# First expert's raw weights and two transposed v tiles in their own slots, loads in another order, key maxima one slot ahead

## The chip, the cores and the metric

The kernel runs on one core of a Trainium2 chip. The metric is the device time of one execution in microseconds (us); the figures are the median and the range of three executions. One more execution was recorded by the hardware profiler. The core has five engines that each work through an instruction stream of their own: TensorE (PE, matmuls), VectorE (DVE), ScalarE (ACT), GpSimd (POOL) and SyncE (SP, which here issues all DMAs, in order). They wait for each other by semaphores.

## The reference

Local attention over 2 x 8 heads, then a mixture of four experts, then a two-matrix layer with a sigmoid gate. All inputs are float32 (the last two matrices arrive as float64).

```python
# attention, per head: 768 queries, head size 64
k_sum = k.reshape(B, H, nb, 32, D).max(axis=3)        # block maxima of the keys
v_sum = v.reshape(B, H, nb, 32, D).mean(axis=3)       # block means of the values
scores_l = where(|i - j| < 16, scale * q @ k.T, -1e9)
scores_s = scale * q @ k_sum.T + log(32)
a = softmax(concat(scores_l, scores_s))               # (its sum + 1e-9)
x = a @ concat(v, v_sum)                              # -> (1536, 512)
# experts: p = domain_probs / (sum + 1e-9)
out = sum over e of p[:, e] * (relu(x @ w1[e]) @ w2[e])     # 512 -> 1024 -> 512
# last layer: h = out @ w_in (512 -> 2048); g = h * sigmoid(1.702 h); result g @ w_out
```

## The kernel before, in words

Heads are handled in pairs (`hp`, four of them), which fill 128 partitions. A *group* is one batch, one pair and four windows of 64 queries; there are 24. Each group passes through a pipeline with one stage a *slot*: `att_a(i)` and `att_b(i)` are slot i. In slot i group i gets its scores (TensorE; VectorE scales them, adds the mask and takes the row maximum), group i-1 is normalised (VectorE sums, GpSimd multiplies), group i-2 is transposed, group i-3 is multiplied with v. `maxima` are the block maxima of a pair's keys, `windows` copies the four key windows and (on GpSimd) the maxima behind them into one tile kw, two slots ahead of use. `fold_v` (GpSimd), `sums` (VectorE) and `means` (TensorE, ScalarE, GpSimd) make the block means of v and put them behind the group's v tile.

A float32 product is made from two parts: hi, rounded to TensorE's format by ScalarE, and lo, the remainder. `split(k, h, hi engine, lo engine)` does this for half h of weight piece k (A = 0: first matrix, C = 1: second); lo is a subtraction of a 128 x 512 tile on GpSimd or VectorE. Each product takes three passes (hi hi, hi lo, lo hi). The first expert has eight pieces, the four experts 32.

The main program starts with ten idle matmuls, then slots 0 to 7. From slot 4 to 7 TensorE also makes the first four hidden tiles, one contraction step a slot (`early`): here xhi, xlo, whi and wlo of pieces 0 to 3 are needed. Behind slot 7 the four are scaled and split by `hidden`, in VectorE's stream ahead of slot 8. From then on each slot has also one unit: twelve matmuls of a hidden tile (`first`), and twelve or 24 of an output (`second`).

The order on each engine is that in which the program text runs. The dictionaries `middle` and `after` say which weight splits and loads belong to which slot. SyncE takes the loads in the order in which they are written; a load whose buffer is still read waits there, and all behind it too. Buffers: q tiles 4, vT tiles 2, vw tiles 5, raw weight halves 5 (each 128 x 512), and a pool of nine slots of 8 KB per partition that the key pairs, xhi and xlo, and later the accumulators use. Beyond 110 us the program only runs units; there `load_w(k + 2)` is called behind the split of piece k.

## Time and profile before

| | |
|---|---|
| median of 3 executions | 893.27 us (892.4 to 895.41) |
| profiled execution | 894.08 us |
| span in the profile (first to last instruction) | 892.3 us |
| TensorE busy | 861.5 us, 97% |
| VectorE / ScalarE / GpSimd busy | 394.9 / 254.6 / 249.8 us |
| mean granted TensorE clock | 0.987 of full speed |
| chain that ended last, by engine | PE 88%, DVE 5%, DMA 4% |

A time in a row is counted from the start of the span. In a timeline the bracket at a row's end gives how long the engine was idle before the instruction and what ended that. A granted clock of 0.50 is TensorE's lower level, 1.2 GHz, and 1.00 the upper, 2.4 GHz.

### The profile page before, as it was taken

The page shows a single profiled execution, that of the slowest core. Times are in us where ns is not written, and L with a number is a line of the kernel's source. Part 1 is how long each engine was busy: PE and PEld are TensorE (multiplying, and loading weights), DVE is VectorE, ACT ScalarE, POOL GpSimd, SP SyncE. Part 2 cuts the span into 40 slices and gives each one's busy share as a digit, 9 for nine tenths or more (in the row PEclk, how much of TensorE's full clock was granted, in tenths as well). Part 3 has the DMA queues.
Part 4 walks back from the last instruction along what each step waited for, and adds up shares of the span by engine and source line. Part 5 has one row for each costly group of instructions (what it writes and reads, how often), then busy time and mean ns, then how long its engine had stood idle before and what let it go on. Part 6 is the DMA issues. An engine that isn't in the chain of part 4 may idle for free.

```text
span 892.3 us, 11708 instructions
## 1 busy us (share of the span) xinstructions
PE 861.5 (97%) x4564; PEld 717.5 (80%) x4564; DVE 394.9 (44%) x684; ACT 254.6 (29%) x586; POOL 249.8 (28%) x261
## 2 busy tenths in 40 slices
PE   6679899999999999999999999999999999999998
PEld 6568788888888888788888888888788888888886
DVE  6457554235555455655455653232322222223233
ACT  3555554123411113211113212123423234322221
POOL 5546432015631115621116613034500014200000
PEclk8889999999999999999999999999999999999999
DMA  7552322204532325542225411003200002001011
GB/s 237 156 191 93 111 66 69 84 12 154 165 107 71 83 80 160 172 120 71 83 71 177 152 50 35 1 14 100 76 0 1 1 25 83 1 1 48 0 48 48
DMA packets 36199, 71.72 MB, mean 80 GB/s; under 512 B 5040, under 2 KB 8368, under 8 KB 36144
## 3 DMA queue, kind: packets, MB, share of 16 engines
q1 hardware_dynamic: 36144, 70.98, 25.4%
q8 instruction: 36, 0.59, 0.3%
q14 instruction: 19, 0.16, 0.1%
HBM read 59.40 MB, written 11.56 MB: 80 GB/s over the span
## 4 chain that ended last, share of the span: by engine, by line
PE 88%; DVE 5%; DMA 4%; ACT 1%; issue 1%; POOL 1%; SPq 0%; DVEq 0%; POOLq 0%; ACTq 0%
PE h L402 42%; PE o L455 41%; PE sc L288 2%; PE xo L338 1%; DMA q<-kq 1%; DMA k<-kq 1%; PE at L326 1%; DVE acc L479 1%; DVE g L420 1%; DVE hl L428 0%; POOL wlo L216 0%; DMA vT<-vT 0%; DVE nm L301 0%; DVE s L296 0%; ACT hh L427 0%
## 5 line engine op out<-in xcount | busy, mean ns | idle before, releaser
L427 ACT CAST hh<-g 128x512 fp32r<-128x512 f32 (+1 forms) x152 | 90.9, 598 | 406.1 <-DVE g L420 369.5
L216 POOL TENSOR_TENSOR wlo<-raw,whi 128x512 fp32r<-128x512 f32 x91 | 121.9, 1363 | 163.3 <-ACT whi L210 155.5
L428 DVE TENSOR_TENSOR hl<-g,hh 128x512 fp32r<-128x512 f32 (+1 forms) x152 | 114.8, 756 | 106.3 <-ACT hh L427 106.3
L402 PE MATMUL h<-xhi,wlo 128*128 128x512 f32 (+1 forms) x416 | 156.1, 375 | 3.0 <-POOL wlo L216 3.0
L402 PE MATMUL h<-xhi,whi 128*128 128x512 f32 (+1 forms) x416 | 158.6, 381 | 0.0
L455 PE MATMUL o<-hh,whi 128*128 128x512 f32 (+1 forms) x416 | 155.6, 374 | 2.1 <-DVE g L420 2.1
L402 PE MATMUL h<-xlo,whi 128*128 128x512 f32 (+1 forms) x416 | 156.0, 375 | 0.0
L455 PE MATMUL o<-hl,whi 128*128 128x512 f32 (+1 forms) x416 | 155.2, 373 | 0.0
L455 PE MATMUL o<-hh,wlo 128*128 128x512 f32 (+1 forms) x416 | 155.1, 373 | 0.0
L420 DVE SCALAR_TENSOR_TENSOR g<-h,pb 128x512 f32<-128x512 f32 (+1 forms) x104 | 67.6, 650 | 175.9 <-PE h L402 175.9
L426 DVE TENSOR_TENSOR g<-h,g 128x512 f32<-128x512 f32 x48 | 33.2, 692 | 155.2 <-ACT g L425 155.2
L402 PEld LDWEIGHTS h<-xhi,wlo 128*128 128x128 f32 x416 | 79.1, 190 | 17.0 <-POOL wlo L216 3.1
L455 PEld LDWEIGHTS o<-hh,whi 128*128 128x128 f32 x416 | 78.4, 188 | 17.3 <-DVE g L420 3.8
L402 PEld LDWEIGHTS h<-xhi,whi 128*128 128x128 f32 x416 | 79.4, 191 | 15.3 <-issue 0.6
L402 PEld LDWEIGHTS h<-xlo,whi 128*128 128x128 f32 x416 | 79.2, 190 | 13.5
L455 PEld LDWEIGHTS o<-hh,wlo 128*128 128x128 f32 x416 | 78.3, 188 | 13.8
L455 PEld LDWEIGHTS o<-hl,whi 128*128 128x128 f32 x416 | 78.4, 188 | 13.7
L193 POOL TENSOR_SCALAR d<-d 128x512 int32<-128x512 int32 x32 | 20.6, 644 | 216.0 <-DVE d L189 216.0
L455 PE MATMUL o<-whi,hh 128*128 128x512 f32 x192 | 74.9, 390 | 0.7 <-DVE g L426 0.7
L402 PE MATMUL h<-yhi,wlo 128*128 128x512 f32 x192 | 74.8, 390 | 0.0
L455 PE MATMUL o<-wlo,hh 128*128 128x512 f32 x192 | 74.8, 389 | 0.0
L402 PE MATMUL h<-ylo,whi 128*128 128x512 f32 x192 | 74.8, 389 | 0.0
(69 smaller groups left out, 987.2 us busy)
## 6 DMA issues: line engine op xcount, KB each, us to landing
raw<-wts SPq DMA_DIRECT2D x64, 256.0 KB, 4.8
d<-w SPq DMA_DIRECT2D x32, 512.0 KB, 4.5
w<-o SPq DMA_DIRECT2D x32, 256.0 KB, 2.3
raw<-w SPq DMA_DIRECT2D x32, 256.0 KB, 2.9
vw<-vw SPq DMA_DIRECT2D x24, 192.0 KB, 3.5
k<-kq SPq DMA_DIRECT2D x8, 400.0 KB, 6.4
q<-kq SPq DMA_DIRECT2D x24, 128.0 KB, 3.4
vT<-vT SPq DMA_DIRECT2D x8, 384.0 KB, 3.5
```

The source lines that it names most:

```text
L193: nc.gpsimd.tensor_scalar(out=lo, in0=lo, scalar1=0.5, scalar2=0.25, op0=ALU.mult, op1=ALU.add)
L216: engine.tensor_tensor(out=wlo[k][:, c], in0=raws[k, h], in1=whi[k][:, c].bitcast(F32), op=ALU.subtract)
L288: nc.tensor.matmul(ps[r, j * KA : (j + 1) * KA], q[r, j * WIN : (j + 1) * WIN], k[r, j, :], start=True, stop=True,)
L326: nc.tensor.transpose(ps[0:KA, j * P : (j + 1) * P], s[:, j, :], ident)
L338: nc.tensor.matmul(ps[h * D : (h + 1) * D, j * WIN : (j + 1) * WIN], v[0:KA, j, h * D : (h + 1) * D], a[0:KA, j * P + h * WIN : j * P + (h ...
L402: nc.tensor.matmul(hid[i][:, 0:n], wt[:, c], xt[:, k, x], start=(k == 0 and m == 0), stop=(k == KC - 1 and m == 2),)
L420: nc.vector.scalar_tensor_tensor(out=g, in0=ps, scalar=0.0, in1=pbs[ph, t][:, c0 : c0 + n], op0=ALU.max, op1=ALU.mult,)
L426: nc.vector.tensor_tensor(out=g, in0=ps, in1=g, op=ALU.mult)
L427: nc.scalar.copy(hh, g)
L428: nc.vector.tensor_tensor(out=hl, in0=g, in1=hh.bitcast(F32), op=ALU.subtract)
L455: nc.tensor.matmul(o, a, b, start=(f == 0 and m == 0), stop=(f == NF - 1 and m == 2))
L479: nc.vector.tensor_tensor(out=o, in0=ps[d][:, 0:n], in1=o, op=ALU.add)
```

## The change

The raw halves of the first expert's pieces 0 to 5 no longer go through the ring of raw tiles but lie in three of the nine slots (`raws0`, `raws2`, `raws4`), and vT of pairs 2 and 3 of the first batch lies in one more (`vT0`). The ring of raw tiles has 4 buffers, was 5; that of q has 6, was 4. The loads are in another order: domain probabilities, pieces 0 to 3's first halves and the first six groups' tiles come in one run at the start, q loads come four slots ahead of use (were two). The maxima and windows of pairs 1 to 3 of the first batch are taken in the slot before they are used. The gates (`gates`) go from slot 3 to slot 2, and some splits go to other slots or from GpSimd to VectorE.

```diff
--- before.py
+++ after.py
@@ -107,7 +107,7 @@
     nc.gpsimd.memset(mask[:, NM - 1, WIN + RAD - 1 : KW], NEG)
 
 
-    kts, ks2, qs, vs, vts = {}, {}, {}, {}, {}
+    kts, ks2, qs, vs, vts, vt2 = {}, {}, {}, {}, {}, []
 
     def load_k(b, hp):
         if hp % 2 == 0:
@@ -117,13 +117,18 @@
 
     def load_q(g):
         b, hp, w0 = g
-        t = att.tile([P, GQ], F32, tag="q", bufs=4, name="q{}{}{}".format(*g))
+        t = att.tile([P, GQ], F32, tag="q", bufs=6, name="q{}{}{}".format(*g))
         c = PAD + w0 * WIN
         nc.sync.dma_start(out=t, in_=kq[b, hp, :, c : c + GQ])
         qs[g] = t
 
     def load_vt(b, hp):
-        t = att.tile([P, S], F32, tag="vT", bufs=2, name=f"vT{b}{hp}")
+        if b == 0 and hp >= 2:
+            if hp == 2:
+                vt2.append(slot([P, 2, S], F32, "vT0"))
+            t = vt2[0][:, hp - 2]
+        else:
+            t = att.tile([P, S], F32, tag="vT", bufs=2, name=f"vT{b}{hp}")
         nc.sync.dma_start(out=t, in_=vT[b, hp])
         vts[b, hp] = t
 
@@ -134,7 +139,8 @@
         vs[g] = t
 
 
-    raws, whi, wlo = {}, {}, {}
+    raws, pairs, whi, wlo = {}, {}, {}, {}
+    NEARLY = 6
     NPIECE = NPH * NF
     N32 = NE * NF
     HALVES = (slice(0, DM), slice(DM, 2 * DM))
@@ -143,8 +149,14 @@
 
     def load_w(k, halves=(0, 1)):
         if k < NPIECE:
+
+            if k < NEARLY and k % 2 == 0 and k not in pairs:
+                pairs[k] = slot([P, 2, 2 * DM], F32, f"raws{k}")
             for h in halves:
-                raws[k, h] = work.tile([P, DM], F32, tag="raw", bufs=5, name=f"raw{k}{h}")
+                if k < NEARLY:
+                    raws[k, h] = pairs[k - k % 2][:, k % 2, HALVES[h]]
+                else:
+                    raws[k, h] = work.tile([P, DM], F32, tag="raw", bufs=4, name=f"raw{k}{h}")
                 assert k < N32 or (k - N32) * 2 + h in parked
                 src = wts[k // NF, k % NF] if k < N32 else w32[k - N32]
                 nc.sync.dma_start(out=raws[k, h], in_=src[:, HALVES[h]])
@@ -511,7 +523,11 @@
             scores(groups[i])
         if 1 <= i <= NG:
             normalise(groups[i - 1])
-        if i + 2 < NG:
+
+        if i + 1 < HP:
+            maxima(*groups[i + 1][:2])
+            windows(groups[i + 1])
+        if HP <= i + 2 < NG:
             windows(groups[i + 2])
         for act in middle.get(i, ()):
             act()
@@ -531,7 +547,7 @@
             exponentials(groups[i])
         if 3 <= i < NG + 3:
             low(groups[i - 3])
-        if opens(i + 3):
+        if opens(i + 3) and i + 3 >= HP:
             maxima(*groups[i + 3][:2])
         for act in after.get(i, ()):
             act()
@@ -539,50 +555,57 @@
     A, C = 0, 1
     act, pool, dve = nc.scalar, nc.gpsimd, nc.vector
     middle = {
-        3: [lambda: split(0, A, act, pool), lambda: split(1, A, act, pool)],
+        3: [lambda: split(0, A, act, pool), lambda: split(1, A, act, dve)],
         4: [lambda: split(2, A, act, pool), lambda: split(3, A, act, dve)],
         5: [lambda: split(0, C, act, pool)],
-        6: [lambda: split(1, C, act, pool)],
-        7: [lambda: split(2, C, act, pool), lambda: split(4, A, act, dve)],
-        8: [lambda: split(3, C, act, pool), lambda: split(5, A, act, dve)],
-        9: [lambda: split(4, C, act, pool), lambda: split(6, A, act, dve)],
-        10: [lambda: split(5, C, act, pool), lambda: split(7, A, act, dve)],
-        11: [lambda: split(6, C, act, pool)],
-        12: [lambda: split(7, C, act, pool)],
+        6: [lambda: split(1, C, act, pool), lambda: split(4, A, act, dve)],
+        7: [lambda: split(2, C, act, pool), lambda: split(3, C, act, dve)],
+        8: [lambda: split(4, C, act, pool), lambda: split(5, A, act, dve)],
+        9: [lambda: split(5, C, act, pool), lambda: split(6, A, act, dve)],
+        10: [lambda: split(6, C, act, pool), lambda: split(7, A, act, dve)],
+        11: [lambda: split(7, C, act, pool)],
     }
     after = {
-        0: [lambda: x_tiles(0, "x"), lambda: load_w(1, (A,))],
-        1: [lambda: load_vt(0, 2), lambda: load_v(groups[2]), lambda: load_w(2, (A,)), gates_load],
-        2: [lambda: load_vt(0, 3), lambda: load_v(groups[3]), lambda: load_w(3, (A,))],
-        3: [gates, lambda: load_p(0, 0)],
-        4: [lambda: x_tiles(1, "x")],
-        8: [lambda: load_p(0, 1)],
+        0: [lambda: x_tiles(0, "x")],
+        2: [gates],
+        5: [lambda: load_p(0, 0)],
+        8: [lambda: x_tiles(1, "x"), lambda: load_p(0, 1)],
         15: [lambda: x_tiles(2, "x")],
     }
 
     def later(i, *acts):
         after.setdefault(i, []).extend(acts)
 
-    order_w = [(0, C), (1, C), (4, A), (2, C), (3, C), (5, A), (4, C), (6, A), (5, C), (7, A),
+    order_w = [(0, C), (4, A), (1, C), (2, C), (3, C), (5, A), (4, C), (6, A), (5, C), (7, A),
                (6, C), (7, C)]
-    at_w = [3, 3, 4, 4, 5, 5, 6, 6, 7, 8, 8, 9]
+    at_w = [0, 0, 1, 1, 2, 2, 3, 4, 4, 5, 5, 6]
     for (k, h), i in zip(order_w, at_w):
         later(i, lambda k=k, h=h: load_w(k, (h,)))
-    for n in range(4, NG):
-        later(n - 2, lambda n=n: load_q(groups[n]), lambda n=n: load_v(groups[n]))
+    for n in range(6, NG):
+        later(max(n - 4, 0), lambda n=n: load_q(groups[n]))
+    for n in range(5, NG):
+        later(n - 2, lambda n=n: load_v(groups[n]))
     for hp in range(HP):
         later(6 + hp // 2, lambda hp=hp: load_k(1, hp))
         later(9 + hp, lambda hp=hp: load_vt(1, hp))
 
-    for hp in range(2):
+    for hp in range(HP):
         load_k(0, hp)
         load_q(groups[hp])
-    for hp in range(2, HP):
-        load_vt(0, hp - 2)
-        load_v(groups[hp - 2])
-        load_k(0, hp)
-        load_q(groups[hp])
+        if hp == 1:
+            gates_load()
+        if hp >= 1:
+            load_vt(0, hp - 1)
+            load_v(groups[hp - 1])
     load_w(0, (A,))
+    load_w(1, (A,))
+    load_vt(0, 3)
+    load_v(groups[3])
+    load_w(2, (A,))
+    load_w(3, (A,))
+    load_q(groups[4])
+    load_v(groups[4])
+    load_q(groups[5])
 
 
     ps = bank(3, "warm")
@@ -594,9 +617,6 @@
     spin(10)
     maxima(0, 0)
     windows(groups[0])
-    maxima(0, 1)
-    windows(groups[1])
-    maxima(0, 2)
     START = 4 + KC
     SPIN = (0, 4, 4, 4)
     for i in range(START):
```

VectorE at the start of the program. In the names the digits are batch, pair and first window (q034 is batch 0, pair 3, window 4); ks are maxima, kw window copies, s scaled scores, nm row maxima. Before:

```order
L244 TENSOR_REDUCE ks00_138<-k00_103 128x24
L256 COPY kw000_140<-k00_103 128x4x96
L244 TENSOR_REDUCE ks01_143<-k00_103 128x24
L256 COPY kw010_145<-k00_103 128x4x96
L244 TENSOR_REDUCE ks02_148<-k02_114 128x24
L296 SCALAR_TENSOR_TENSOR s000_159<-sc000_150,mask_79 128x480
L301 TENSOR_REDUCE nm000_161<-s000_159 128x4
L256 COPY kw020_163<-k02_114 128x4x96
L244 TENSOR_REDUCE ks03_172<-k02_114 128x24
L296 SCALAR_TENSOR_TENSOR s010_187<-sc010_178,mask_79 128x480
L301 TENSOR_REDUCE nm010_189<-s010_187 128x4
```

Changed:

```order
L256 TENSOR_REDUCE ks00_156<-k00_103 128x24
L268 COPY kw000_158<-k00_103 128x4x96
L308 SCALAR_TENSOR_TENSOR s000_170<-sc000_161,mask_79 128x480
L313 TENSOR_REDUCE nm000_172<-s000_170 128x4
L256 TENSOR_REDUCE ks01_174<-k00_103 128x24
L268 COPY kw010_176<-k00_103 128x4x96
L308 SCALAR_TENSOR_TENSOR s010_199<-sc010_190,mask_79 128x480
L313 TENSOR_REDUCE nm010_201<-s010_199 128x4
L328 TENSOR_SCALAR sm000_180<-sm000_180 128x4
L329 RECIPROCAL sm000_180<-sm000_180 128x4
L256 TENSOR_REDUCE ks02_206<-k02_115 128x24
L268 COPY kw020_208<-k02_115 128x4x96
```

The scaling of group 000 and its maximum went ahead of ks01; ks02, which stood ahead of the first scaling, comes behind the sums of slot 1, and ks03 (beyond the rows shown) behind those of slot 2.

SyncE's queue for slots 3 to 5 (raw40 is the first half of piece 4, pb the broadcast gate). Before:

```order
L150 DMA raw11_338<-wts 128x512
L122 DMA q014_340<-kq 128x256
L133 DMA vw014_342<-vw 96x512
L150 DMA raw40_418<-wts 128x512
L150 DMA raw21_420<-wts 128x512
L122 DMA q024_422<-kq 128x256
L133 DMA vw024_424<-vw 96x512
L150 DMA raw31_487<-wts 128x512
L150 DMA raw50_489<-wts 128x512
L122 DMA q034_491<-kq 128x256
L133 DMA vw034_493<-vw 96x512
L150 DMA raw41_552<-wts 128x512
```

Changed:

```order
L383 DMA pscr_101<-dp_102 128x4x12
L162 DMA raws2_136<-wts 128x512
L162 DMA raws4_188<-wts 128x512
L122 DMA q024_279<-kq 128x256
L162 DMA raws4_188<-wts 128x512
L122 DMA q034_343<-kq 128x256
L138 DMA vw014_345<-vw 96x512
L162 DMA raw60_419<-wts 128x512
L162 DMA raws4_188<-wts 128x512
L122 DMA q008_422<-kq 128x256
L138 DMA vw024_424<-vw 96x512
L389 DMA pb00_487<-pscr_101 128x512
```

The q loads of groups 024, 034 and 008 stand behind loads into slots of their own, where they stood behind loads into the raw ring.

SyncE's queue around the second batch's vT loads. Before:

```order
L127 DMA vT11_914<-vT 128x768
L122 DMA q110_994<-kq 128x256
L133 DMA vw110_996<-vw 96x512
L127 DMA vT12_998<-vT 128x768
L122 DMA q120_1077<-kq 128x256
L133 DMA vw120_1079<-vw 96x512
L127 DMA vT13_1081<-vT 128x768
L122 DMA q130_1159<-kq 128x256
L133 DMA vw130_1161<-vw 96x512
```

Changed:

```order
L132 DMA vT11_910<-vT 128x768
L122 DMA q130_990<-kq 128x256
L138 DMA vw110_992<-vw 96x512
L132 DMA vT12_994<-vT 128x768
L122 DMA q104_1071<-kq 128x256
L138 DMA vw120_1073<-vw 96x512
L132 DMA vT13_1075<-vT 128x768
L122 DMA q108_1153<-kq 128x256
L138 DMA vw130_1155<-vw 96x512
```

The vT loads kept their places; q120 and q130 are now ahead of vT12, and q104 and q108 are behind it.

## Rows read from the trace of the kernel before

**Rows 1.** Windows: stretch, its length, busy us of each engine (instructions), PEclk, DMA share, GB/s.
```profile
0.00:110.00 110.00, 85.82 (x874) 75.93 (x875) 63.21 (x147) 56.03 (x196) 56.25 (x80) 0.89 0.51 158
5.70:11.20 5.50, 1.07 (x19) 0.86 (x18) 2.83 (x5) 0.00 (x0) 0.85 (x3) 0.79 1.05 337
54.25:58.20 3.95, 3.95 (x37) 3.19 (x37) 2.50 (x8) 2.03 (x4) 0.18 (x1) 0.50 0.89 301
100.62:104.60 3.98, 3.98 (x39) 3.22 (x40) 2.28 (x6) 0.88 (x2) 0.59 (x1) 0.57 0.30 99
110.00:892.30 782.30, 775.69 (x3693) 641.55 (x3691) 331.74 (x538) 198.59 (x391) 193.51 (x181) 1.00 0.22 69
```

**Rows 2.** Timeline of TensorE: start, duration, instruction, count, idle before and releaser.
```profile
5.71 1.04 PE L288 MATMUL sc<-kw,q 64*64 64x120 f32 x16
11.18 1.87 PE L288 MATMUL sc<-kw,q 64*64 64x120 f32 x16 [4.43 <-DVE s L296]
...
32.54 0.43 PE L402 MATMUL h<-xhi,wlo 128*128 128x256 f32 x1 [2.95 <-POOL wlo L216]
...
44.77 1.04 PE L288 MATMUL sc<-kw,q 64*64 64x120 f32 x16 [1.16 <-DMA q<-kq]
...
54.25 1.86 PE L288 MATMUL sc<-kw,q 64*64 64x120 f32 x16 [5.76 <-DMA q<-kq]
...
65.02 0.69 PE L338 MATMUL xo<-aT,vw 120*64 120x64 f32 x16
...
93.21 1.04 PE L288 MATMUL sc<-kw,q 64*64 64x120 f32 x16 [1.58 <-DMA q<-kq]
...
100.62 1.54 PE L288 MATMUL sc<-kw,q 64*64 64x120 f32 x16 [2.05 <-DMA q<-kq]
```

**Rows 3.** Timeline of SyncE's queue, at the third vT load.
```profile
89.35 0.33 SPq L127 DMA_DIRECT2D vT<-vT  x1
89.73 0.43 SPq L122 DMA_DIRECT2D q<-kq  x1
```

**Rows 4.** Timeline of VectorE, in slots 1, 3 and behind slot 7.
```profile
13.03 0.95 DVE L244 TENSOR_REDUCE ks<-k 128x24 f32<-128x768 f32 x1 [0.91 <-DMA k<-kq]
13.90 0.65 DVE L296 SCALAR_TENSOR_TENSOR s<-sc,mask 128x480 f32<-128x480 f32 x1
14.58 0.65 DVE L301 TENSOR_REDUCE nm<-s 128x4 f32<-128x480 f32 x1
15.15 0.16 DVE L316 TENSOR_SCALAR sm<-sm 128x4 f32<-128x4 f32 x1
...
15.44 0.33 DVE L256 COPY kw<-k 128x384 f32<-128x384 f32 x1
...
23.00 0.23 DVE L365 TENSOR_REDUCE ds<-dp 128x12 f32<-128x48 f32 x1
...
24.29 0.96 DVE L368 TENSOR_TENSOR dp<-dp,ds 128x48 f32<-128x48 f32 x1
...
54.89 0.42 DVE L428 TENSOR_TENSOR hl<-g,hh 128x256 fp32r<-128x256 f32 x1 [0.47 <-ACT hh L427]
```

**Rows 5.** Timeline of GpSimd, in slots 3 and 8.
```profile
21.55 0.99 POOL L318 TENSOR_TENSOR s<-s,sm 128x480 f32<-128x480 f32 x1
22.48 0.26 POOL L257 COPY kw<-ks 128x96 f32<-128x96 f32 x1
22.70 2.49 POOL L216 TENSOR_TENSOR wlo<-raw,whi 128x512 fp32r<-128x512 f32 x2
25.14 1.00 POOL L238 TENSOR_TENSOR vT<-vT 128x384 f32<-128x384 f32 x1
26.21 0.61 POOL L277 COPY vw<-vm 24x512 f32<-24x512 f32 x1
...
58.02 1.52 POOL L318 TENSOR_TENSOR s<-s,sm 128x480 f32<-128x480 f32 x1 [6.68 <-DVE sm L317]
...
61.07 0.61 POOL L277 COPY vw<-vm 24x512 f32<-24x512 f32 x1
```

## The prediction

> **What bounds the kernel now.** I read the windows by stretch first: they say where TensorE is idle. It is busy 85.82 of the first 110 us and 775.69 of the other 782.3 [rows 1]. So 24.2 of the 30.8 idle microseconds lie before 110 us, and nothing that the change does there can be worth more than these and what a halved clock costs beside them. Next I read TensorE's timeline up to 110 us, where each row names the wait ahead of it. The reader is to see, besides shorter ones, seven waits [rows 2]: 4.43 us until VectorE scaled the first scores, 2.95 us for a weight remainder (wlo) from GpSimd, and five for a q tile, of which the four shown are 1.16, 5.76, 1.58 and 2.05 us. Third comes SyncE's queue, which issues all loads in order. A vT load at 89.35 us stands ahead of a q load at 89.73 us, for which the score matmuls of 93.21 us wait [rows 2, 3]; the wait that ends at 100.62 us repeats it one slot later. The q tile is late because something in front of it in the queue waits for a buffer. Last come VectorE and GpSimd, whose instructions per slot become the bound once the loads are gone [rows 4, 5].
>
> **The early slots.** VectorE now scales group 0's scores right after the first maxima, where it did the maxima of heads 1 and 2 first. The first score matmuls still start at 5.71 and end at 6.75 us, so their scaling starts at 6.77. From start to start rows 4 give: scaling to maximum 0.68, maximum to sum 0.57, sum to the following work 0.29, key maxima to window copy 0.87 (13.03 to 13.90), copy to the next 0.25. So key maxima of head 1 begin at 6.77 + 0.68 + 0.57 = 8.02, their window copy at 8.89, and with GpSimd's 0.26 copy behind the maxima the second scores start at 9.35, not at 11.18.
> From there one slot is a closed ring: scaling, maximum, sum, GpSimd's normalisation (0.99, it begins some 0.5 after the sum) and its 0.26 copy put the next scores 3.05 behind the scaling, and the scores take 1.04 at full clock and 1.87 after the long idle [rows 2]. That is 4.15 or 4.95 a slot. Group 1 is scaled at 10.4 to 11.25 (I take 10.9), group 2 at 14.5 to 16.2 (15.1).
> Slot 2 has two window copies, the v sum and now also the four gate operations, all in front of group 3's scaling. They start at 15.1 + 0.68 + 0.57 + 0.29 + 0.87 + 2 x 0.25 + 0.46 = 18.47 and took 2.25 (23.00 to 25.25) [rows 4], so group 3 is scaled at 20.7, although its scores are done at 19.2. The gates cost 1.5 there. Slot 3's sum is at 22.0 and the normalisation of group 2 at 22.5.
> Then GpSimd is the bound: normalise 0.99, copy 0.26, remainder 1.25 (one now, the second goes to VectorE), v sum 1.00, v mean 0.61, normalise 0.99, copy 0.26, remainder 1.25 [rows 5]: 6.61, so 29.1 us. As normalisations also take 1.52, I take 29.5 for the remainder that TensorE had at 32.5. **Term 1: 3.0 saved**; with the ring at its two ends and two long normalisations 1.5 to 4.0.
> All loads are hidden there. Up to the fourth weight piece the queue holds 5.6 MB by the tiles' sizes; at the 337 GB/s of the busy stretch [rows 1] they have landed by about 19, and the pieces are asked for at 20 to 25. The second key pair's last tile had landed by 13.03 [rows 4]; it is asked for at 17. The raw weights' buffers cost nothing else: they lie in slots that hold nothing before 60 us.
>
> **Slots 4 to 7** repeat the old ones, shifted: between the waits that end at 32.54 and 44.77 us the timeline shows none, and the order within a slot is the same. The q tiles of groups 4 to 7 are now loaded ahead of blocked weight loads, so the wait of 1.16 goes. **Term 2: 1.2** (0 to 1.2; at 0 if another operand is late as well).
>
> **Slot 8.** The 5.76 us wait goes too, and with it half clock: 0.50 for 3.95 us [rows 1], worth 2.0. But then VectorE is late. It is busy with the four first hidden tiles, whose last remainder began at 54.89 and ends at 55.3 [rows 4]; shifted by terms 1 and 2 (4.2) that is 51.1. Only then come group 8's scaling and, 0.68 + 0.57 later, the sum of group 7 at 52.4; GpSimd's normalisation starts at 52.9. From there to the end of the v means took 61.07 + 0.61 - 58.02 = 3.66 [rows 5], so the xo matmuls of slot 9 start at 56.6, where they started at 65.02 [rows 2]. Total so far 8.4, less 4.2: **term 3: 4.2**. Bounds: 7.8 with no such hole (5.76 + 2.0), 1.6 if the holes of 1 to 1.5 us that it leaves ahead of at and xo halve the clock as long as the old one did.
>
> **Slots 14 to 16.** q is loaded four slots ahead. The queue then reaches q120 and q130 before the vT12 load that waits for VectorE's sum, and what now stands behind vT12 is q104, needed two slots later than q120 was; a slot is 5.4 us (100.62 - 93.21 - 2.05), the landing 3.4 (89.73 to 93.1) [rows 2, 3]. Both waits, 1.58 and 2.05, go, and the clock of 0.57 over 3.98 us behind the second [rows 1], worth 1.4 to 1.7. **Term 4: 5.1** (0 if the queue stays blocked, as in the rival below).
>
> **Beyond 110 us** nothing is forecast. The ring of raw tiles is 4, was 5; TensorE idles 6.6 us in 782 there [rows 1], so an issue that is one remainder (1.25) later has cover, and if that were gone it is the price of the last rival.
>
> Sum: 3.0 + 1.2 + 4.2 + 5.1 = 13.5. The profiled execution took 894.08 (span 892.3 and 1.8 around it): 880.6. It lay 0.8 above the median of 893.27, so for the median 879.8; I say 880.
>
> The clock is where rows and a rule part. A 1.16 us gap left the clock alone (the scores behind it took 1.04), gaps of 4.43 and 5.76 halved it (1.87 and 1.86) [rows 2]; the new gaps of 1 to 3.3 us lie between, and I count them at full clock but for the middle value in slot 1. The Trainium skill, "TensorE: Matmul & The Clock Gate" (Part 1, "HAM oscillation"), says that waits between short bursts of matmuls bring the half clock back each time, which speaks against a start with more and shorter gaps. By that rule the time is the second rival's.
>
> **Rivals.**
> 1. *No holes in slots 8 and 9*: VectorE and GpSimd keep up, term 3 is 7.8. For it: before, neither made TensorE wait there. Against: their time there was hidden by the 5.76. 13.5 + 3.6 = 17.1: 876.2.
> 2. *The new gaps halve the clock*: scores of 1.87 in slots 1 and 2 (group 2 at 16.2, term 1 at 1.9) and half clock after the holes (term 3 at 1.6). For it: 4.43 did so. Against: 1.16 did not. 1.9 + 1.2 + 1.6 + 5.1 = 9.8: 883.5.
> 3. *The queue stays blocked*: it doesn't do what it says. v tiles wait for their readers in the same queue (PE xo), and each load waits for the one eight before it, so the new order only moves the block; term 4 is 0 and 8.4 is left: 884.9. Against: the last v load ahead of q120 waits for the xo matmuls of slot 9, five slots before q120 is needed.
> 4. *Slower: the raw ring.* From the eighth piece on each half load waits for the subtraction of the tile four before it, SyncE stands still meanwhile, and stores and loads of the conversion behind it slip until TensorE waits for remainders. Each that shows costs 1.25; there are 80. It decides from 11 on (11 x 1.25 = 13.7 eats the gain); with 20, 894.08 - 13.5 + 25 = 905.6. Against: TensorE had no such wait beyond 110 us.
>
> **Chances.** Forecast (gain 11 to 16) 0.54; rival 1 0.16; rival 2 0.16; rival 3 0.08; rival 4 0.03; a loss of most of the gain to something unseen 0.03. Measurement can tell 0.3%, 2.7 us, from no change. Faster by more: the first four and a part of the rest, 0.94; same 0.03, slower 0.03. The range takes in rivals 1 to 3 with term 1's ends: 875 to 887.
>
> **What would show it.** In the changed profile: second scores near 9.4 and group 3's scaling behind the gates near 21; the remainder wait ending near 29.5; the scores of slot 8 near 44, with no q wait from there to 110 us; gaps of 1 to 2 us ahead of at and xo near 52 to 57 with GpSimd named; no wait near 80 to 95 and a clock of 1.00 there; and from the place that was 110 us to the end the same 782 us. I am wrong if a q or vT transfer still ends a wait, if half clock lies over the stretch of 45 to 60, or if TensorE waits for a wlo beyond 110 us.

## The result, and the profile after

The changed kernel takes 882.17 us (median of 4 runs, 881.78 to 882.47); the kernel before, run beside it, 893.92 (892.4 to 895.41). The ratio is 0.9868 [0.985, 0.9887]. The forecast was 880.0 in a range of 875 to 887. The profiled execution took 882.47 with a span of 880.7, where it was 892.3: 11.6 less.

The windows of the changed kernel answer to [rows 1], in the same columns: the first 110 us, three stretches in it, and the rest.

```profile
0.00:110.00 110.00, 94.35 (x1004) 83.72 (x1005) 72.20 (x168) 63.04 (x226) 59.50 (x85) 0.94 0.56 167
10.00:14.00 4.00, 3.61 (x24) 3.21 (x24) 1.87 (x6) 1.08 (x7) 1.24 (x3) 0.57 1.06 314
30.00:34.00 4.00, 3.14 (x25) 2.69 (x25) 0.00 (x0) 0.58 (x1) 0.80 (x1) 0.50 0.58 174
58.00:62.00 4.00, 4.00 (x29) 3.93 (x26) 3.06 (x8) 2.31 (x11) 3.14 (x4) 0.57 0.57 183
110.00:880.70 770.70, 764.04 (x3562) 630.62 (x3560) 324.26 (x518) 191.00 (x362) 189.10 (x175) 1.00 0.22 69
```

TensorE is now busy 94.35 of the first 110 us, where it was 85.82; beyond 110 it idles 6.66 us, where it was 6.6. All the gain lies before 110 us. At 58 to 62, behind the xo matmuls of slot 9, the clock is 0.57 although TensorE is busy throughout; that is new, since the kernel before had 1.00 behind these matmuls (65 to 69 us).

TensorE's timeline of the changed kernel, answering to [rows 2] (start, duration, instruction, count, idle before and its releaser):

```profile
5.93 1.60 PE L300 MATMUL sc<-kw,q 64*64 64x120 f32 x16
10.39 1.77 PE L300 MATMUL sc<-kw,q 64*64 64x120 f32 x16 [2.87 <-POOL kw L269]
...
15.44 1.04 PE L300 MATMUL sc<-kw,q 64*64 64x120 f32 x16 [1.32 <-POOL kw L269]
...
19.75 1.04 PE L300 MATMUL sc<-kw,q 64*64 64x120 f32 x16 [1.64 <-DMA raws<-wts]
...
30.86 0.58 PE L414 MATMUL h<-xhi,wlo 128*128 128x256 f32 x1 [3.50 <-POOL wlo L228]
...
41.89 1.04 PE L300 MATMUL sc<-kw,q 64*64 64x120 f32 x16
...
48.96 0.69 PE L350 MATMUL xo<-aT,vw 120*64 120x64 f32 x16 [1.53 <-POOL vw L289]
...
57.61 0.69 PE L350 MATMUL xo<-aT,vw 120*64 120x64 f32 x16 [1.54 <-POOL vw L289]
...
64.22 1.04 PE L300 MATMUL sc<-kw,q 64*64 64x120 f32 x16
...
95.73 1.04 PE L300 MATMUL sc<-kw,q 64*64 64x120 f32 x16
```

All five waits for a q tile are gone; the wait for a remainder (wlo) of 3.50 us remains and ends at 30.86. In slots 1 to 3 the scores wait 2.87, 1.32 and 1.64 us for the copy of their window (kw); the last of these is put down to a weight load, which scores don't read, and in the profiles of two of the kernels below the same 1.64 us is put down to kw. In slots 8 and 9 the xo matmuls wait 1.53 and 1.54 us for GpSimd's v means (vw), as the prediction's step on slot 8 had it. From slot 10 to slot 16 no score matmul waits.

To read the gain off such timelines I take the same instruction of both kernels and subtract the starts. Two of before's starts were not among the rows ahead of the prediction (70.14 and 107.40), nor were two waits that turn out to matter (3.39 and 0.43); here they are, from the timeline of TensorE before.

```profile
25.85 1.84 PE L288 MATMUL sc<-kw,q 64*64 64x120 f32 x16 [3.39 <-DMA q<-kq]
...
70.14 1.04 PE L288 MATMUL sc<-kw,q 64*64 64x120 f32 x16
...
87.87 0.69 PE L338 MATMUL xo<-aT,vw 120*64 120x64 f32 x16 [0.43 <-POOL vw L277]
...
107.40 1.04 PE L288 MATMUL sc<-kw,q 64*64 64x120 f32 x16
```

| Place | before | after | earlier by | of this new | forecast |
|---|---|---|---|---|---|
| the wlo wait ends | 32.54 | 30.86 | 1.68 | 1.7 (term 1) | 3.0 |
| scores of slot 7 | 44.77 | 41.89 | 2.88 | 1.2 (term 2) | 1.2 |
| scores of slot 10 | 70.14 | 64.22 | 5.92 | 3.0 (term 3) | 4.2 |
| scores of slot 16 | 107.40 | 95.73 | 11.67 | 5.75 (term 4) | 5.1 |
| the end of the span | 892.3 | 880.7 | 11.6 | -0.1 | 0 |

VectorE in the changed kernel, answering to [rows 4]: the scalings of groups 0 and 3, the last gate operation, the weight remainder of piece 1, and the last hidden remainder ahead of group 8's scaling.

```profile
7.66 0.66 DVE L308 SCALAR_TENSOR_TENSOR s<-sc,mask 128x480 f32<-128x480 f32 x1 [2.47 <-PE sc L300]
...
21.25 0.40 DVE L380 TENSOR_TENSOR dp<-dp,ds 128x48 f32<-128x48 f32 x1
21.58 0.65 DVE L308 SCALAR_TENSOR_TENSOR s<-sc,mask 128x480 f32<-128x480 f32 x1
...
23.36 0.68 DVE L228 TENSOR_TENSOR wlo<-raws,whi 128x512 fp32r<-128x512 f32 x1
...
51.70 0.43 DVE L440 TENSOR_TENSOR hl<-g,hh 128x256 fp32r<-128x256 f32 x1 [0.47 <-ACT hh L439]
52.04 0.65 DVE L308 SCALAR_TENSOR_TENSOR s<-sc,mask 128x480 f32<-128x480 f32 x1
```

GpSimd in the changed kernel, answering to [rows 5]: its run up to the remainder that TensorE waits for, and slot 8.

```profile
23.37 1.52 POOL L330 TENSOR_TENSOR s<-s,sm 128x480 f32<-128x480 f32 x1 [1.78 <-ACT xhi L359]
...
28.07 1.31 POOL L330 TENSOR_TENSOR s<-s,sm 128x480 f32<-128x480 f32 x1
...
29.55 1.26 POOL L228 TENSOR_TENSOR wlo<-raws,whi 128x512 fp32r<-128x512 f32 x1
...
53.84 1.52 POOL L330 TENSOR_TENSOR s<-s,sm 128x480 f32<-128x480 f32 x1 [4.94 <-DVE sm L329]
...
56.86 0.69 POOL L289 COPY vw<-vm 24x512 f32<-24x512 f32 x1
```

The order of events is the predicted one with a start 0.9 late: group 0 is scaled at 7.66 (forecast 6.77), group 3 at 21.58 (20.7). GpSimd's run from the normalisation at 23.37 to the end of the remainder at 30.81 takes 7.4 us, where the forecast had 6.6 plus 0.4 of allowance, because both normalisations are long ones (1.52 and 1.31). Each starts while VectorE subtracts a weight remainder, as the first does at 23.37 against 23.36. So it is in both traces up to 110 us: all 11 normalisations longer than 0.99 us (5 before, 6 changed) start beside such a remainder, and none of the 22 that took 0.99 does. Moving piece 1's remainder to VectorE took 1.25 off GpSimd's run, as the forecast has it, and the normalisation beside it grew by 0.53.

### The profile page after: what moved, and what is told of

The parts are those of the page before. It is cut to its first block, busy times and chain, and to the rows that moved or that the text cites. A ratio compares the mean times of both kernels' runs of the same rounds, so it can differ in the third digit from the quotient of the medians.

```text
span 880.7 us, 11689 instructions
## 1 busy us (share of the span) xinstructions
PE 858.4 (97%) x4564; PEld 714.3 (81%) x4564; DVE 396.5 (45%) x686; ACT 254.0 (29%) x586; POOL 248.6 (28%) x259
## 4 chain that ended last, share of the span: by engine, by line
PE 90%; DVE 4%; DMA 2%; ACT 1%; POOL 1%; issue 1%; SPq 0%; DVEq 0%; POOLq 0%; ACTq 0%
PE h L414 43%; PE o L467 42%; PE sc L300 2%; PE xo L350 2%; DMA q<-kq 1%; PE at L338 1%; DVE acc L491 1%; DVE g L432 1%; DVE hl L440 1%; DMA raws<-wts 1%; ACT hh L439 1%; POOL wlo L228 0%; DVE o L185 0%; DVE d L198 0%; ACT yhi L493 0%
## 5 line engine op out<-in xcount | busy, mean ns | idle before, releaser
L228 POOL TENSOR_TENSOR wlo<-raw,whi 128x512 fp32r<-128x512 f32 x82 | 110.5, 1372 | 163.6 <-ACT whi L222 158.7
L414 PE MATMUL h<-yhi,whi 128*128 128x512 f32 x192 | 74.7, 389 | 0.0
```

What stands on the lines that cost most here:

```text
L228: engine.tensor_tensor(out=wlo[k][:, c], in0=raws[k, h], in1=whi[k][:, c].bitcast(F32), op=ALU.subtract)
L414: nc.tensor.matmul(hid[i][:, 0:n], wt[:, c], xt[:, k, x], start=(k == 0 and m == 0), stop=(k == KC - 1 and m == 2),)
```

## The experiments

Each kernel was timed in 5 rounds beside the kernel before, and the ratios below are to that kernel. Diffs are against the changed kernel unless said otherwise. The changed kernel was run a second time among them.

> The changed kernel as it is, on the same chip as the others of this call: 882.2.

It took 881.6 us (880.56 to 882.56), 0.9863 [0.9842, 0.9884], and its profile repeats the first one, with 0.57 at 58 to 62 us again. So a difference of some 2 us between two kernels of the following cannot be told by time alone, and for these the trace is read.

**q two slots ahead again, late slots only.** This tests term 4.

```diff
-        later(max(n - 4, 0), lambda n=n: load_q(groups[n]))
+        later(n - 4 if n < 12 else n - 2, lambda n=n: load_q(groups[n]))
```

> The changed kernel, with the q loads of the second batch's groups two slots ahead again (were four). My theory: term 4 was the q loads' place ahead of vT12 and vT13, so the waits ahead of the scores of slots 14 and 15 and the half clock behind them come back: 5.0 to 5.8 us slower than the changed kernel's 882.2, so about 887.6, with all before slot 12 unchanged. Rival: the waits went because the raw weight loads no longer block the queue; then nothing changes, 882.2.

Measured: 886.52 us (885.24 to 887.09), 0.9912 [0.9895, 0.993]. TensorE's timeline of this kernel, slots 14 to 16:

```profile
85.83 1.06 PE L300 MATMUL sc<-kw,q 64*64 64x120 f32 x16 [2.47 <-DMA q<-kq]
86.82 1.10 PE L338 MATMUL at<-ident,s 128*120 128x128 f32 x4
...
93.23 1.04 PE L300 MATMUL sc<-kw,q 64*64 64x120 f32 x16 [0.61 <-DMA q<-kq]
...
98.52 1.04 PE L300 MATMUL sc<-kw,q 64*64 64x120 f32 x16
```

The waits for q are back (2.47 and 0.61), and with them a half clock: over 86 to 90 us it is 0.59, and the at matmuls of slot 14 take 1.10 us where the changed kernel's take 0.65. From the scores of slot 13 to those of slot 16 it takes 98.52 - 78.05 = 20.47 us, where three slots of the changed kernel take 95.73 - 79.91 = 15.82: 4.65 us by the trace, of which the two waits are 3.08 and the rest, some 1.6, goes with the clock; by the times it is some 4, under the 5.0 to 5.8 that I expected. Term 4 is the lead of the q loads, as forecast.

**Only the lead of the q loads, on the kernel before.** The rival to terms 1 to 3: not the storage and the early maxima, but the q loads alone. The diff is against the kernel before; the raw ring gives up the buffer that the two more q tiles need.

```diff
-        t = att.tile([P, GQ], F32, tag="q", bufs=4, name="q{}{}{}".format(*g))
+        t = att.tile([P, GQ], F32, tag="q", bufs=6, name="q{}{}{}".format(*g))
...
-                raws[k, h] = work.tile([P, DM], F32, tag="raw", bufs=5, name=f"raw{k}{h}")
+                raws[k, h] = work.tile([P, DM], F32, tag="raw", bufs=4, name=f"raw{k}{h}")
...
-        later(n - 2, lambda n=n: load_q(groups[n]), lambda n=n: load_v(groups[n]))
+        later(max(n - 4, 1), lambda n=n: load_q(groups[n]))
+        later(n - 2, lambda n=n: load_v(groups[n]))
```

> The kernel before, with one part of the change alone: q loads four slots ahead of use (behind the v load of the slot), six q buffers, four raw ones. My theory: term 4 comes whole (5.0 to 5.8), terms 2 and 3 in part, since q still stands behind raw loads that wait for the ring, but two slots earlier: 1.2 + 3.0 = 4.2 more; term 1 not at all: 893.9 - 9.5 = 884.5. Rival: without slots of their own for the raw weights the queue is as blocked as before up to slot 8, and only term 4 comes: 888.5.

Measured: 882.07 us (881.43 to 883.18), 0.9876 [0.9854, 0.9897], 2.4 less than I expected and the same as the whole change. TensorE's timeline of this kernel:

```profile
22.57 1.04 PE L288 MATMUL sc<-kw,q 64*64 64x120 f32 x16 [0.74 <-DVE xlo L352]
...
29.78 0.58 PE L402 MATMUL h<-xhi,wlo 128*128 128x256 f32 x1 [4.53 <-POOL wlo L216]
...
41.94 1.04 PE L288 MATMUL sc<-kw,q 64*64 64x120 f32 x16
...
48.91 0.69 PE L338 MATMUL xo<-aT,vw 120*64 120x64 f32 x16 [1.53 <-POOL vw L277]
...
57.56 0.69 PE L338 MATMUL xo<-aT,vw 120*64 120x64 f32 x16 [1.54 <-POOL vw L277]
...
62.68 1.04 PE L288 MATMUL sc<-kw,q 64*64 64x120 f32 x16
...
94.68 1.04 PE L288 MATMUL sc<-kw,q 64*64 64x120 f32 x16
```

It still does its first maxima in the old order and keeps the raw weights in the ring, yet the wlo wait ends at 29.78, earlier than in the changed kernel. The reason stands at slot 4: the scores of 25.85 us before had waited 3.39 for their q tile, and they start at 22.57 here. What hangs on them shows on VectorE and GpSimd in the kernel before, and then on GpSimd in this one:

```profile
27.73 0.66 DVE L296 SCALAR_TENSOR_TENSOR s<-sc,mask 128x480 f32<-128x480 f32 x1 [2.48 <-PE sc L288]
```

```profile
29.54 1.52 POOL L318 TENSOR_TENSOR s<-s,sm 128x480 f32<-128x480 f32 x1 [2.72 <-DVE sm L317]
...
31.23 1.26 POOL L216 TENSOR_TENSOR wlo<-raw,whi 128x512 fp32r<-128x512 f32 x1
```

```profile
26.78 1.52 POOL L318 TENSOR_TENSOR s<-s,sm 128x480 f32<-128x480 f32 x1 [0.41 <-DVE sm L317]
...
28.47 1.26 POOL L216 TENSOR_TENSOR wlo<-raw,whi 128x512 fp32r<-128x512 f32 x1
```

Before, GpSimd stood still 2.72 us for the sums (sm) of group 3, which VectorE takes behind its scaling of group 4, and that waits for the late scores; here it waits 0.41. So the remainder that ended TensorE's wait was late because of a q tile. Slots 7 to 9 then repeat the changed kernel's, the same holes in slots 8 and 9 included; slot 10 starts 1.5 us earlier (62.68 against 64.22), since the clock is 1.00 over 58 to 62 here.

**All but the lead of the q loads.** The counterpart. The q tiles of groups 4 and 5 still come in the first run of loads, so the 3.39 us wait of slot 4 is not put to the test here.

```diff
-        later(max(n - 4, 0), lambda n=n: load_q(groups[n]))
+        later(n - 2, lambda n=n: load_q(groups[n]))
```

> The changed kernel with all its parts but one: every q load two slots ahead of use, as before (the tiles of groups 0 to 5 still in the first run of loads). My theory after the run with the q loads alone (882.07): the two parts are two cures of the same waits up to slot 8, since a q load behind weight loads that have slots of their own is not blocked either, and only the q order cures slots 14 and 15. So this is as the kernel with the second batch's q two ahead, 886.5. Rival: without q four ahead the waits of slots 7 and 8 come back as well (6.9 us and 2 for the clock): 893 or more.

Measured: 886.79 us (886.09 to 887.29), 0.992 [0.9902, 0.9939], as expected. Its wlo wait ends at 30.85 and its slot 7 scores start at 41.86, like the changed kernel's; slot 14 waits 2.30 and slot 15 0.68 us for q. So for the q waits of slots 7 and 8 there are two cures: let the q loads go first, or give the loads that they stand behind a place that is free at once. The q loads alone bring 893.3 - 882.1 = 11.2 us, the rest alone 894.0 - 886.8 = 7.2, both together some 12. Some 6 us are counted in both.

**The maxima in front again.** Is the early scaling worth anything by itself?

```diff
-        if i + 1 < HP:
-            maxima(*groups[i + 1][:2])
-            windows(groups[i + 1])
-        if HP <= i + 2 < NG:
+        if i + 2 < NG:
...
-        if opens(i + 3) and i + 3 >= HP:
+        if opens(i + 3):
...
+    maxima(0, 1)
+    windows(groups[1])
+    maxima(0, 2)
```

> The changed kernel, with the first groups' maxima and windows back where they were: maxima of heads 0 to 2 ahead of the first scaling, windows two slots ahead. My theory, from the ring of 4.3 us a slot that I measure now (scalings at 7.66, 12.20, 16.51, 21.58) against 10.43, 13.90, 16.38, 18.98 before: one slot ahead loses by slot 3 what it won in slot 0, so undoing it starts group 3's scaling 1 to 2 us earlier and the time is 880.5 to 881.5. The claim of my prediction's term 1 is the rival: the early first scaling is worth its 3 us, undoing it is 2 to 3 us slower, 884 to 885.

Measured: 882.8 us (881.43 to 882.93), 0.9865 [0.9847, 0.9884]. Group 0 is scaled at 11.98 instead of 7.66, but group 3 at 22.14 instead of 21.58, and the wlo wait ends at 31.42 instead of 30.86. Of the 4.3 us lead at group 0 0.6 is left three groups later, and the time doesn't show it. Neither expectation held: the part costs nothing and brings nothing that can be measured.

**The gates in slot 4 instead of slot 2.**

```diff
-        2: [gates],
+        4: [gates],
```

> The changed kernel, with the gates in slot 4 (was 2), where VectorE idles from 29 to 34 us. My theory: the four gate operations cost 0.8 us in front of group 3's scaling (20.79 to 21.58), and all of it reaches the weight remainder that TensorE waits for, so that wait ends at 30.0 instead of 30.86: 881.4. Rival: GpSimd is the bound there by itself (the normalisation of group 2 starts at 23.37 whatever VectorE does), nothing changes: 882.2.

Measured: 881.47 us (880.08 to 882.01), 0.9852 [0.9833, 0.9871]. From group 2's scaling to group 3's it takes 20.45 - 16.14 = 4.31 us instead of 21.58 - 16.51 = 5.07: the gates cost 0.76 there, half of the forecast 1.5. The wlo wait ends at 29.74, 1.12 earlier, of which 0.37 is an earlier start of this execution. The trace agrees with the theory; the time cannot tell.

**Remainder 2 on VectorE.**

```diff
-        4: [lambda: split(2, A, act, pool), lambda: split(3, A, act, dve)],
+        4: [lambda: split(2, A, act, dve), lambda: split(3, A, act, dve)],
```

> The changed kernel; the remainder of weight piece 2 in slot 4 is made on VectorE, not GpSimd. My theory: what was left of term 1 is GpSimd's run of 7.4 us from the normalisation of group 2 to this remainder; without it the 3.50 us wait ends some 2.0 to 2.5 earlier: 880.0. Rival: the next thing (xo's v means on GpSimd, or the second operand) is late right behind it, and TensorE gains 0.5 at most: 881.7.

Measured: 880.32 us (879.6 to 881.2), 0.9855 [0.9834, 0.9876]. TensorE's timeline of this kernel:

```profile
28.57 0.58 PE L414 MATMUL h<-xhi,wlo 128*128 128x256 f32 x1 [1.22 <-DVE wlo L228]
...
29.96 0.58 PE L414 MATMUL h<-xhi,wlo 128*128 128x256 f32 x1 [0.38 <-DVE wlo L228]
```

The wait of 3.50 us is now two, 1.22 and 0.38, and the xo matmuls behind them start at 31.33 instead of 32.86. GpSimd's serial run was what set the end of the wait in the changed kernel, as term 1's last step says. In the time it is 1 to 2 us, which the rounds don't settle.

**The v means ahead of the pool splits.** For the holes in slots 8 and 9 the theory was that GpSimd's remainder in front of the v means makes them.

```diff
-        7: [lambda: split(2, C, act, pool), lambda: split(3, C, act, dve)],
-        8: [lambda: split(4, C, act, pool), lambda: split(5, A, act, dve)],
+        7: [lambda: split(3, C, act, dve)],
+        8: [lambda: split(5, A, act, dve)],
...
-        8: [lambda: x_tiles(1, "x"), lambda: load_p(0, 1)],
+        7: [lambda: split(2, C, act, pool)],
+        8: [lambda: split(4, C, act, pool), lambda: x_tiles(1, "x"), lambda: load_p(0, 1)],
```

> The changed kernel, with GpSimd's weight subtractions of slots 7 and 8 behind the v means of these slots instead of ahead. My theory: the two waits of xo for the means (1.53 and 1.54) go or shrink by 1.27 each, and with them the half clock of 58.2 to 61.7 us, which cost 1.6 to 1.8: 882.2 - 2.5 - 1.7 = 878.0. Rival: the half clock comes from the earlier gaps together and stays: 879.7. Rival: the normalisation is late by itself and nothing changes: 882.

Measured: 882.31 us (881.65 to 882.8), 0.9863 [0.9845, 0.9881]. The xo matmuls wait 0.23 and 0.69 instead of 1.53 and 1.54, but nothing is won. ScalarE and then TensorE in this kernel's timeline:

```profile
48.58 0.60 ACT L222 CAST whi<-raws 128x512 fp32r<-128x512 f32 x1
49.09 0.40 ACT L439 CAST hh<-g 128x256 fp32r<-128x256 f32 x1
```

```profile
52.51 0.39 PE L467 MATMUL o<-hh,whi 128*128 128x256 f32 x1 [0.61 <-DVE g L432]
```

The whole split moved, its rounding on ScalarE (whi, 0.60 us) with it, and that now stands ahead of the rounding of the first hidden tile (hh). The second products then wait for hidden tiles (g), 0.61 and 0.62, and at waits 0.51 for GpSimd's s; group 8 is scaled at 54.50 instead of 52.04, of which 1.0 was there at slot 7 (42.89 against 41.89). From the scores of slot 8 to those of slot 10 it takes 63.73 - 46.67 = 17.06 us at a clock of 1.00 over 58 to 62; the kernel with q two slots ahead late, with the old holes at that clock, takes 17.06 too. So the waits for the means shrank as the theory has it, but the edit put as much elsewhere, and doesn't settle what GpSimd's part alone is worth. The next suspect for slot 8 is the run of hidden tiles over VectorE and ScalarE in turn, 1.23 us each.

**The hidden tiles interleaved.** The next expectation follows from that: take the next tile's gating (g) ahead of the last one's remainder (hl), so that VectorE has work while ScalarE rounds.

```diff
+    def hidden_b(i):
+        g, hh, hl = pend.pop(i)
+        nc.vector.tensor_tensor(out=hl, in0=g, in1=hh.bitcast(F32), op=ALU.subtract)
+        hid[i] = (hh, hl)
...
-        hidden(i)
+        hidden_a(i)
+        if i:
+            hidden_b(i - 1)
+    hidden_b(EARLY - 1)
```

> The changed kernel; of the four first hidden tiles, VectorE makes the next tile's product ahead of the last one's remainder, so it no longer waits for ScalarE's rounding (1.05 and 3 x 0.47 us). My theory: group 8's scaling and with it the normalisation of group 7 and the v means that xo waits for are bound by this serial run; all of it comes about 1.5 to 1.9 us earlier, the waits ahead of at and xo in slots 8 and 9 shrink by that: 882.2 - 1.7 = 880.5, and up to 1.6 less where the half clock of 58 to 62 us goes with them. Rival: the wait is GpSimd's own (subtraction of a weight and normalisation in front of the means), nothing changes: 882.2.

Measured: 879.37 us (879.15 to 881.41), 0.9849 [0.9827, 0.987]. VectorE and then TensorE in this kernel's timeline:

```profile
50.47 0.65 DVE L308 SCALAR_TENSOR_TENSOR s<-sc,mask 128x480 f32<-128x480 f32 x1
```

```profile
56.04 0.69 PE L350 MATMUL xo<-aT,vw 120*64 120x64 f32 x16 [0.37 <-POOL vw L289]
...
61.16 1.04 PE L300 MATMUL sc<-kw,q 64*64 64x120 f32 x16
```

Group 8 is scaled 1.57 us earlier, the second hole shrinks from 1.54 to 0.37, and the scores of slot 10 start at 61.16 instead of 64.22: 1.57 from the serial run and 1.5 from a clock that stays at 1.00 over 58 to 62. The first is confirmed: from the scores of slot 8 to those of slot 10 it takes 61.16 - 45.64 = 15.52 us, 1.54 less than the 17.06 of the kernel with the old holes at the same clock. The clock's 1.5 can't be put down to the edit, since that kernel has it without.

**Four edits together.** The interleaving, the gates in slot 4, remainder 2 on VectorE, and of the two splits of the v-means experiment only GpSimd's half behind the means, the rounding where it was. The interleaving's own lines are those shown above.

```diff
-        4: [lambda: split(2, A, act, pool), lambda: split(3, A, act, dve)],
+        4: [lambda: split(2, A, act, dve), lambda: split(3, A, act, dve)],
...
-        7: [lambda: split(2, C, act, pool), lambda: split(3, C, act, dve)],
-        8: [lambda: split(4, C, act, pool), lambda: split(5, A, act, dve)],
+        7: [lambda: split_hi(2, C, act), lambda: split(3, C, act, dve)],
+        8: [lambda: split_hi(4, C, act), lambda: split(5, A, act, dve)],
...
-        2: [gates],
+        4: [gates],
...
-        8: [lambda: x_tiles(1, "x"), lambda: load_p(0, 1)],
+        7: [lambda: split_lo(2, C, pool)],
+        8: [lambda: split_lo(4, C, pool), lambda: x_tiles(1, "x"), lambda: load_p(0, 1)],
```

> The changed kernel with four edits together: gates in slot 4, the four first hidden tiles interleaved, remainder of piece 2 on VectorE, and GpSimd's subtractions of slots 7 and 8 behind the v means with ScalarE's rounding left in its place. By the single runs: 0.7 + 2.0 to 2.8 + 1.9 less than 882.2, and 1.2 for the xo wait of slot 8 that is left: 876.2. Rival: these waits hide one another and only the largest counts: 879.4.

Measured: 877.71 us (875.65 to 877.76), 0.9808 [0.9784, 0.9832]; the changed kernel beside it 881.6. Slot 10's scores start at 59.47, the xo matmuls wait 0.23 twice, and the at matmuls ahead of the second 0.88 for GpSimd's s. The time lies between the expected 876.2 and the rival's 879.4: the gains add up in part. It beats both kernels.

**And the maxima of pairs 2 and 3 two slots ahead, behind the window copies.** This comes on top of the four edits; the diff shows only what is added.

```diff
-            maxima(*groups[i + 1][:2])
+            if i == 0:
+                maxima(*groups[1][:2])
...
+            if i + 2 < HP:
+                maxima(*groups[i + 2][:2])
```

> The kernel with the four edits, and the maxima of pairs 2 and 3 two slots ahead, but behind the window copies, so that they stand outside the ring from scaling to scores. My theory: the ring of 4.3 us a slot falls by 0.87 in slots 2 and 3, group 3's scaling comes 1.7 earlier, 1.0 to 1.7 of it reach the first hidden tiles: 875. Rival: the key tiles of pairs 2 and 3 have not landed and hold VectorE, as in the kernel with the maxima in front (first scaling at 11.98): same as with the four edits or up to 1 slower.

Measured: 877.3 us (877.05 to 877.68), 0.9815 [0.9795, 0.9835]: the same. The rival was right: the maxima now wait for their key tiles (0.90 and 0.57), and the scores of slots 1 and 2 take 1.86 at half clock. Group 3 is scaled at 20.95 us, with the four edits alone at 20.82.

## Why the prediction was right or wrong

**The size** came out 1.75 us short, 11.75 at the median where 13.5 was summed. The q waits went at the places named, the two holes came as forecast, and the shorter gaps at the start were there (2.87, 1.32 and 1.64 ahead of scores, 1.10 for a remainder; the forecast had gaps of 1 to 3.3). Measured against the sum, term 1 lacks 1.3 and term 3 1.2, and term 4 has 0.65 more, so in part misses cancel.

**Term 1** is the step that failed, in its size and in its cause. Of its 3.0 us 1.7 were had. The size: the step says "The first score matmuls still start at 5.71 and end at 6.75". They start at 5.93 and take 1.60, so group 0 is scaled 0.9 late and group 2 1.4; the gates gave half a microsecond back (0.8 instead of 1.5), and GpSimd's run took 7.4, 0.4 over the 7.0 that the step allowed, with two normalisations made long beside VectorE's remainders. In the kernel with q two slots ahead in the late slots, which has the same early slots and started at 5.57 with scores of 1.04, the wait ends at 29.22, within the forecast. The cause: the step goes from group 0's early scaling down to GpSimd. But the kernel with only the q loads moved has none of that and its wait ends at 29.78, and with the maxima in front again only 0.56 is lost. What held the remainder before was the wait of 3.39 us for group 4's q tile. I had counted it among the five q waits and gave it no term; the prediction follows GpSimd's rows [rows 5] up to its mean at 26.21 and doesn't ask why its next instruction starts at 29.54. That term 1 came out within its 1.5 to 4.0 all the same is luck: the part it names brought some 0.6, and a wait that it doesn't price the rest.

**Term 2** is right, size and mechanism: 1.2.

**Term 3** has the mechanism and too large a size. Up to the xo matmuls of slot 9 the forecast total was 8.4, and it is 65.02 - 57.61 = 7.41, so the term is 4.5 there. Its steps hold, all 0.9 to 1.0 late, which term 1's miss of 1.3 covers: the last hidden remainder is done at 52.1 (forecast 51.1), the normalisation starts at 53.84 (52.9), and from there to the end of the means it is 56.86 + 0.69 - 53.84 = 3.71 us (3.66). Then 1.5 us are given back, as the clock is 0.57 over 58 to 62: from the scores of slot 8 to those of slot 10 it takes 18.55 us, and 17.06 in the kernel with q two slots ahead late, with the same holes (1.54, 0.30 and 1.54) at a clock of 1.00. The step's lower bound of 1.6 lies 2.6 under its 4.2, though it prices a half clock as long as the old one at 2.0; with that the bound is 2.2 and the second rival's time 0.6 less.

**Term 4** is right in mechanism and 0.65 too small. Its price was read from the two waits and the half clock behind the second; a wait of 0.43 us for the v means in slot 13 (87.87) went too, which the changed kernel doesn't have; putting the q loads back cost 4.65, a half clock of some 1.6 included.

**The rivals.** *No holes* is wrong: the holes came, where and as large as the sum had them. *Half clock behind the new gaps* is in good part right, and its 883.5 lies nearer to the measured 882.2 than the forecast does: a half clock followed the holes ahead of 58 us, and these 1.5 us are the largest of the misses; in slot 1 the scores took 1.77, near its 1.87, but in slot 2 1.04. One sign of being wrong that the prediction names came in part, since the half clock of 58 to 62 begins inside its 45 to 60. *Queue stays blocked* is wrong: a vT load stands ahead of a q load at 83.8 us as before, but it is the q of a later slot. *The raw ring* is wrong: beyond 110 us there is no wait for a remainder, and the kernel that has only the q order, with a ring of 4, shows none either.

**The rule on the clock.** Over 10 to 14 us the granted clock is 0.57 and over 30 to 34 it is 0.50, behind waits of 2.87 and 3.50 us, and at 58 to 62 it is 0.57 behind waits of 1.5, 0.3 and 1.5. Behind the waits of 1.32 and 1.64 us it stays up: over 14 to 18 it is 1.00, and the scores take 1.04. The Trainium skill, "TensorE: Matmul & The Clock Gate" (Part 1, "HAM oscillation"), has waits between short bursts bring the half clock back each time; in its example the wait is longer than the burst. The changed kernel's trace agrees with it behind its longest waits and not behind those of 1.32 and 1.64, and in the kernel with q two slots ahead late a wait of 2.86 us left the clock at 1.00 over 10 to 14. Ahead of 58 us seven of the profiles have the same three waits. In five (the changed kernel twice, the maxima in front, the gates in slot 4, all but the q lead) the scores behind the wlo wait had taken 1.04 to 1.25 and 58 to 62 ran at 0.57 to 0.65; in two (q two slots ahead late, only the q lead) they had taken 1.86 and 1.87 and it ran at 1.00. What decides between them stays open.

What also stays open is the storage by itself. A kernel with the ring for the first pieces but the new order of loads wasn't tried: those loads would wait for splits that come behind them in the program.

## What to carry to other kernels

In a queue that issues in order, ask of each late tile which load in front of it waits for a buffer: moving the late loads two slots forward was here worth as much as the whole change (11.2 us), and more than the new storage and the other parts without it (7.2). When two parts of a change cure the same wait, run each alone, since the sum of their prices isn't theirs to have. And when an engine's run of work seems to bound a stage, look for the idle time inside that run first: here 2.72 us on GpSimd led back to a q tile.

## What the hardware did that I had not expected

- The half clock moved from one place to another between kernels with nearly the same waits. In the changed kernel the scores behind the wlo wait (34.31 us) took 1.07, and 58 to 62 ran at 0.57. In the two kernels with q two slots ahead late and with only the q lead the same scores took 1.86 and 1.87, and 58 to 62 ran at 1.00. The first of them, q two slots ahead late, left that wait 1.64 us earlier and reached slot 7 only 0.37 earlier. Its timeline:

```profile
5.57 1.04 PE L300 MATMUL sc<-kw,q 64*64 64x120 f32 x16
...
29.22 0.58 PE L414 MATMUL h<-xhi,wlo 128*128 128x256 f32 x1 [3.25 <-POOL wlo L228]
...
32.68 1.86 PE L300 MATMUL sc<-kw,q 64*64 64x120 f32 x16
...
41.52 1.04 PE L300 MATMUL sc<-kw,q 64*64 64x120 f32 x16
...
57.24 0.69 PE L350 MATMUL xo<-aT,vw 120*64 120x64 f32 x16 [1.54 <-POOL vw L289]
...
62.36 1.04 PE L300 MATMUL sc<-kw,q 64*64 64x120 f32 x16
```

- The first scores took 1.60 us in the changed kernel and 1.04 with q two slots ahead late, with a granted clock of 1.00 over 6 to 10 us in both. The warm-up matmuls ahead of them took 4.64 and 4.12, but with the gates in slot 4 scores of 1.13 followed a warm-up of 4.64.
- The same instruction has two prices: GpSimd's normalisation 0.99, or 1.52 where it starts with a weight remainder on VectorE; VectorE's hidden remainder 0.43 (51.70 us), or 1.43 (55.65 us) where GpSimd has been subtracting a weight since 55.53; the last gate operation 0.40 (21.25 us) or 0.96 [rows 4].
